# An attention-then-MLP kernel: four 64x64 transposes at a time, beta's transpose moved back, and a planner with other ScalarE and VectorE times

## The chip, the cores and the metric

The kernel runs on one core of one Trainium2 chip. The metric is the device time of one execution in microseconds (us); the time of the kernel before is the median of three runs, 304.22 us (304.19, 304.22 and 305.46). About 0.5% (1.5 us) is what a measurement of this kernel can tell from no change.

A core has TensorE (PE; its weight loads are shown apart as PEld), VectorE (DVE), ScalarE (ACT), GpSimd (POOL) and SyncE (SP), each with its own queue of instructions that run in order. Engines wait for one another by semaphores. POOL and SP issue nearly all DMAs here.

## The reference

Sliding-window attention over 8 batches and 8 heads (576 positions of 64 elements), followed by an MLP with a gated activation on the 4608 resulting tokens:

```python
scores = scale * np.matmul(q, k.transpose(0, 1, 3, 2))
mask_plain = (rel >= 0) & (rel < window)                                  # heads 0 to 3, window 32
mask_dil = (rel >= 0) & (rel < window * dilation) & (rel % dilation == 0) # heads 4 to 7, dilation 4
attn = softmax(scores where the mask holds)
x = np.matmul(attn, v), heads side by side: [4608, 512]
h = x @ w_in                                                              # [4608, 2048]
g = h * (1.0 / (1.0 + np.exp(-beta * h)))
out = g @ w_out                                                           # [4608, 512]
```

## The kernel before

The MLP is done in 9 tiles of 512 tokens. For a tile, the first product (line 868) makes 16 blocks of hidden units with four matmuls each; ACT takes a tanh of each block (line 877, scaled by half of beta), DVE forms the gate (line 882), and the second product (line 903) makes four blocks of 128 tokens with 16 matmuls each, which go out by way of `osb`. Input arrives in `xT`, the attention's output with features on partitions. Attention runs one batch at a time; batch b must be done before the tiles of tokens that it covers. For the first two batches `xT` is made by PE transposes (lines 807, 822 and 837), later by DMA.

For the first three batches (`DIRECT = 3`) keys and queries are loaded by DMA with a cast to bf16 into `st`, then transposed on PE, and copied out of PSUM by ACT or DVE:

- the dilated heads 4 to 7 (names KD0, KD1, QD0, QD1) by six transposes of 96 rows each (line 466) into `dk` and `dq`;
- the plain heads 0 to 3 (KP0, KP1, QP0, QP1) by 18 transposes each of a 64x64 piece (line 473) into `kT` and `qT`. Index i in 0 and 1 picks a pair of heads; the two heads of a pair lie on partitions 0 to 63 and 64 to 127 of `st`, and stay there in the output. KP0 and KP1 are two planned steps, each with its own PSUM bank.

Scores are made for the dilated heads at line 664, for the tail of the sequence at line 633 and for the plain heads at line 728; ACT takes the exponentials (line 600); values follow at lines 769, 785 and 754, and DVE divides by the sums (lines 619 and 620) into `xdm`, `xsp` and `xdt`. In batch 0 the mask is added in PSUM by matmuls with an identity (lines 654, 714 and 717); in the others it is multiplied after the exponential, on POOL or DVE (line 604).

The first keys (dilated, batch 0) come by SP's queue in float32 into the space of `g` and are cast by ACT and DVE; beta follows on the same queue. All other loads of the first 60 us go through POOL's queue in the order of its instructions: queries and keys of batch 0, its values, `w_in` in three parts, keys and queries of batch 1, `w_out` in two parts (8 of the 16 weight blocks each), and then values of batch 1 and the loads of batch 2.

No order is written by hand. A planner (`Plan`, above line 175) holds every step as an operation with a cost per engine, its dependencies and a due time `vt`. It walks through a modelled time: an engine is free again when its last operation has used up its cost (`free[e] = s + d`), and among the steps that can start then, the one that is due first is issued. `NUDGE` shifts the start that the planner sees for single steps, by the step's number, and so changes its choices. Where PE would stand idle by the plan, it puts in a filler matmul on zeros (line 1015). What comes out is a fixed order on each engine; on the chip each instruction runs when its engine reaches it and its semaphores allow it. The planner's costs are not times of the chip, and a change of any cost can move work in the whole program.

Beta's 16x128 array is transposed by one PE instruction (line 951), which needs its DMA and a small identity (`ident_f`) that POOL makes; DVE halves the result (line 953). Its due time of -1.4 lets the planner place it early: ahead of the batch 0 additions at line 654 and of all transposes of keys.

Of the kernel before, what the change touches and what calls it, by code (L numbers as in the profile page):

```python
# [36 lines left out]
class Plan:  # L37
# [3 lines left out]

    CAPS = {"h": 3, "p": 4, "o": 2, "z": 4, "a": 8, "s": 5, "w": 6}
    SWITCH = 95
    NUDGE = {32: -900, 54: 400, 98: -900, 188: -60, 192: -150, 263: -400, 287: 400, 292: -400, 294: 60,
        296: -150, 299: -60, 313: 900, 338: -400, 369: -150, 403: 400, 411: 900, 424: 400, 427: -150,
        527: -400, 770: -150, 970: -900, 977: -900, 988: -400, 1057: -60}
    LAT = {"PE": 210, "ACT": 45, "DVE": 45, "POOL": 60, "SP": 0}
    NEAR = {"PE": 40, "ACT": 60, "DVE": 60, "POOL": 60, "SP": 0}

    def __init__(self, banks):  # L50
# [9 lines left out]
    def run(self, filler=None, filler_until=0.0):  # L60
# [36 lines left out]
        while n_left:  # L97
            best = None
            near = {}
            for o in avail:  # L100
                base = o.ready
                at = {e: max([free[e], base] + [t for x, t in o.group.read.items() if x != e]
                             if o.group is not None and e != "PE" else [free[e], base]) for e, d in o.engs}
                if o.sbuf:
                    at = {e: max(t, port["DVE" if e == "POOL" else "POOL"]) for e, t in at.items()}
                fin = min(at[e] + d for e, d in o.engs)
                for e, d in o.engs:
                    start = at[e]
                    if start + d > fin + 100:
                        continue  # L110
                    if o.dma and len(lanes[e]) >= 8:
                        start = max(start, lanes[e][-8])
                    if o.acquire is not None:
                        start = bank_at(o.acquire, start)
                        if start is None:
                            continue
                    near.setdefault(e, []).append((start, o, d))
            picks = []
            for e, c in near.items():
                first = min(s + o.bias for s, o, _ in c)  # L120
                s, o, d = min((x for x in c if x[0] + x[1].bias <= first + self.NEAR[e]), key=lambda x: (x[1].vt, x[0]))
                picks.append((s, o.vt, e, o, d))
            assert picks, "no work can start"
            s, _, e, o, d = min(picks, key=lambda x: (x[0], x[1]))
            if filler is not None and s <= filler_until and free["PE"] + 300 < s:
                now = free["PE"]
                open_banks = {x.bank for x in held.values()}
                spare = [b for b, t in bank_free.items() if b not in open_banks and t <= now]
                if spare:
                    filler(max(spare, key=lambda b: -bank_free[b]))  # L130
                free["PE"] = now + 225
                halves = False
                continue
            for g in o.acquire or ():
                open_banks = {x.bank for x in held.values()}
                g.bank = min((b for b, t in bank_free.items() if b not in open_banks and t <= s + 1e-6),
                             key=lambda b: -bank_free[b])
                held[id(g)] = g
                g.left = len(g.users)
            o.fn(e)  # L140
            if e == "PE" and o.halves != halves:
                halves = o.halves
                d += self.SWITCH
            free[e] = s + d
            if o.sbuf:
                port[e] = s + d
            o.start, o.end = s, s + d + self.LAT[e]
            if o.group is not None and e != "PE":
                o.group.read[e] = o.end
            if o.dma:  # L150
                at = max(dma_free[e], s + d + 900)
                other = max(dma_free.values()) - at
                dma_free[e] = at + o.dma + max(0.0, min(o.dma, other))
                o.end = dma_free[e] + (o.lat or 1100)
                lanes[e].append(o.end)
            avail.remove(o)
            n_left -= 1
            for x in o.next:
                x.waits -= 1
                x.ready = max(x.ready, o.end)  # L160
                if not x.waits:
                    avail.append(x)
            for g in list(held.values()):
                if o in g.users:
                    g.left -= 1
                    if not g.left:
                        del held[id(g)]
                        g.release = max(u.end for u in g.users)
                        bank_free[g.bank] = g.release
                        ends.append(g)  # L170
            ends[:] = [g for g in ends if g.release > s - 5000]
# [9 lines left out]
def kernel(  # L181
# [10 lines left out]
    nc = tc.nc  # L192
# [199 lines left out]
    def load(queue, args, deps, vt, kb, rate=.4, issue=750, lat=1100):  # L392
        return plan.op(
            [(queue, issue)],
            lambda e: dma(queue, *args), deps, vt, dma=kb * 1024 / rate / 1000, lat=lat)

    def direct_qk(b, z, h0, deps, vt):
        rows, n, dst = ((2 * GD, RD, std) if h0 else (P, RP, stp))
        src = bass.AP(tensor=(k, q)[z].tensor, offset=(k, q)[z][b, h0].offset,
                      ap=[[n * D, rows], [2 * S * D, 2], [1, n * D]])  # L400
        return load("POOL", (dst[z], src), deps, vt, 576, .41 if b else .33, lat=1100 if b else 1500)

    def first_keys():

# [53 lines left out]

    def t_transposes(g, z, kind, i):
        if kind == "D":
            tp = bank(g, BF16)[:, 0:S].rearrange("p (s x g) -> p s x g", s=3, x=2)
            for s_ in range(3):
                for x in range(2):
                    nc.tensor.transpose(tp[:, s_, x], std[z][:, x, (2 * s_ + i) * P:(2 * s_ + i + 1) * P],  # L466
                                        ident_b[0:2 * GD, 0:2 * GD])
        else:
            tp = bank(g, BF16)[:, 0:S].rearrange("p (j g) -> p j g", j=RP)
            for j in range(RP):  # L470
                for h in range(2):
                    rows = slice(64 * h, 64 * h + 64)
                    nc.tensor.transpose(tp[rows, j], stp[z][rows, i, j * D:(j + 1) * D], ident_b[rows, rows])  # L473

    def at_once(x, i, h):

# [13 lines left out]
            last[key] = []  # L490

    xcopy = []

    def back_dma(b, j, vt_of, vdone):

# [33 lines left out]
    def attention(b, ld, names, vts):  # L529
# [2 lines left out]
        vt_of = dict(zip(names, vts))  # L532
        kv = b % 2
        if b < DIRECT:
            for n in [x for x in names if x[0] in "KQ"]:
                z, kind, i = "KQ".index(n[0]), n[1], int(n[2])
                vt = vt_of[n]
                g = Group("a")
                srcs = ld["qk", z, 0 if kind == "P" else 4]
                srcs = srcs if isinstance(srcs, list) else [srcs]  # L540
                tr = plan.op([("PE", (18 * mm(64) if kind == "P" else 6 * mm(QT)))],
                             lambda e, g=g, z=z, kind=kind, i=i: t_transposes(g, z, kind, i),
                             srcs + [ident], vt, acquire=g)
                used(("st", z), tr)
                def evac(e, g=g, z=z, kind=kind, i=i):
                    tp = bank(g, BF16)[:, 0:S]
                    if kind == "P":
# [11 lines left out]

        def mixed(e):  # L560
            copy(e, dkt[kv], dk[kv][:, :, :, CT - KTL:].rearrange("p r h k -> p h k r"))
        o = plan.op([("DVE", 450), ("POOL", 550)], mixed,
                    (steps["KD0"] + steps["KD1"] if b < DIRECT else ready["D"][0:1]) + war(("dkt", kv)), vt_of["T"] - .01, sbuf=True)
        used(("dk", kv, 0), o)
        used(("dk", kv, 1), o)
# [31 lines left out]
        def exp_and_mask(key, sop, g, vt, n, sc, w, m, tiles):  # L597
# [4 lines left out]
            if b >= ADDED or key == ("T",):  # L602
                def mask(e):
                    E[e].tensor_tensor(out=w(), in0=w(), in1=m(), op=ALU.mult)  # L604
                ex = plan.op([("POOL", 170 + 2.2 * n), ("DVE", 160 + .8 * n)], mask,
                             [ex] + [mask_tail if key == ("T",) else mask_ops["D" if key[0] in (2, 3) else "n"]],
                             vt, sbuf=True)
            wrote(*tiles)
# [16 lines left out]
        for name in [n for n in names if n[0] in "ST"]:  # L625
# [112 lines left out]
            for n, x in enumerate(xs):  # L738
                for h in range(2):
                    exp_and_mask((x, j, h), sop, gs[2 * n + h], vt, 3 * QT,  # L740
                                 lambda g=gs[2 * n + h]: bank(g)[:, 0:3 * QT].rearrange("p (a n) -> p a n", a=3),
                                 lambda x=x, j=j, h=h: pt[x][:, 6 * j:6 * j + 6].rearrange(
                                     "p (a h) n -> p h a n", h=2)[:, h, :, 0:QT],
                                 lambda j=j: mask_n[:, 1 + j:4 + j],
                                 [("pt", x, i) for i in range(3 * j, 3 * j + 3)])
        for name in [n for n in names if n[0] in "VU"]:
# [211 lines left out]
    vts = [-3 + 2 * i / len(first) for i in range(len(first))] + [-3, -2.5]  # L958
    vts[first.index("T"):len(first)] = [.2,.35,.45,.5]
    attention(0, ld[0], names0, vts)  # L960

    def xready(lo, hi, kts=range(NKT)):
        return [o for ks, a, b, o in xcopy if a < hi and b > lo and set(kts) & set(ks)]
# [85 lines left out]
```

The softmax here doesn't subtract the row's maximum and nothing guards it: scores larger than these inputs give would overflow.

## Time and profile before

| what | value |
|---|---|
| median of the runs | 304.22 us |
| span of the profiled execution, first to last instruction | 302.8 us |
| PE busy | 292.8 us, 97% |
| DVE busy | 187.8 us, 62% |
| ACT busy | 170.3 us, 56% |
| POOL busy | 88.5 us, 29% |
| DMA moved | 41.98 MB |

The profile gives one execution's span; the runs' times also hold what lies around the span, 1.4 us by the median. A row of a timeline gives the start in us from the span's start, the time it took, engine, source line, operation, out<-in by the program's names, shapes and how many instructions were merged; in brackets the engine's idle time before it and what ended it. A matmul's time holds the way through the array, so merged rows overlap a little. Some matmul records are missing in a trace: a row of 7 matmuls at line 868 can stand for 8.

### The profile page before, as it was taken

Reading aid. Unit: us, or ns where it says so; the run is one execution under the profiler, and the core shown is the slowest. Engines: PE = TensorE matmul, PEld = TensorE weight load, DVE = VectorE, ACT = ScalarE, POOL = GpSimd, SP = SyncE. Lnnn points to the kernel's source line nnn. Section 1 sums busy time; section 2 is a strip of 40 time slices with the busy share of each in tenths; the row PEclk is TensorE's granted clock in tenths of the full one; section 3 lists DMA queues with packets and bytes.
Section 4 is the critical chain, followed back from the end, with each engine's and each line's share of the span. In section 5 each row is a group of like instructions: output and inputs, shape, how many; then the busy total and the mean of one; then the engine's idle time right before and its main releaser. Section 6 shows DMA issues by size and latency. Waiting matters only on the chain.

```text
span 302.8 us, 5972 instructions
## 1 busy us (share of the span) xinstructions
PE 292.8 (97%) x2271; PEld 150.7 (50%) x2307; DVE 187.8 (62%) x424; ACT 170.3 (56%) x306; POOL 88.5 (29%) x126
## 2 busy tenths in 40 slices
PE   7989999999999999999999999999999999999995
PEld 4756555544554444445544454455544444444454
DVE  4777877688867837777677467577746544343300
ACT  3658974856745737383476447646465544554411
POOL 8997263762236137200631055200000000000000
PEclk9999999999999999999999999999999999999999
DMA  7999999799769999995699989996160100010122
GB/s 161 182 209 202 206 177 211 140 133 176 197 153 190 181 213 168 179 187 130 107 189 164 160 208 184 144 212 163 27 167 1 37 36 35 35 37 35 52 86 71
DMA packets 111248, 41.98 MB, mean 139 GB/s; under 512 B 87620, under 2 KB 104596, under 8 KB 111220
## 3 DMA queue, kind: packets, MB, share of 16 engines
q0 software_dynamic: 60336, 18.58, 58.7%
q1 hardware_dynamic: 50740, 22.95, 35.5%
q8 instruction: 18, 0.29, 0.4%
q10 hardware_dynamic: 144, 0.07, 0.1%
q14 instruction: 10, 0.08, 0.1%
HBM read 37.76 MB, written 18.87 MB: 187 GB/s over the span
## 4 chain that ended last, share of the span: by engine, by line
PE 89%; DVE 6%; issue 2%; DMA 1%; ACT 0%; SPq 0%; DVEq 0%
PE bank L903 40%; PE bank L868 39%; DVE g L882 2%; PE bank L785 2%; DMA beta_row<-in_moe_beta_dram 1%; PE bank L664 1%; PE bank L769 1%; PE bank L692 1%; PE bank L466 1%; PE bank L473 1%; DVE xdm L620 1%; DVE ptt L604 1%; PE bank L654 1%; PE bank L754 1%; PE bank L728 1%
## 5 line engine op out<-in xcount | busy, mean ns | idle before, releaser
L877 ACT ACTIVATE tnh<-bank,beta_half 128x512 bf16<-128x512 f32 x144 | 97.6, 690 | 71.4 <-PE bank L868 68.6
L903 PE MATMUL bank<-w_out_bf,g 128*128 128x512 bf16 (+2 forms) x588 | 136.2, 367 | 1.6 <-issue 0.8
L868 PE MATMUL bank<-xT,w_in_bf 128*128 128x512 bf16 (+1 forms) x568 | 136.1, 376 | 1.0 <-issue 0.2
L882 DVE SCALAR_TENSOR_TENSOR g<-tnh,bank 128x512 bf16<-128x512 bf16 x144 | 97.3, 686 | 62.2 <-ACT tnh L877 61.4
L868 PEld LDWEIGHTS <-w_in_bf 128*128 128x128 bf16 x584 | 55.4, 98 | 61.8 <-issue 0.4
L903 PEld LDWEIGHTS <-g 128*128 128x128 bf16 x608 | 54.9, 98 | 56.5
L918 ACT ACTIVATE osb<-bank 128x512 f32<-128x512 f32 (+1 forms) x34 | 20.0, 588 | 31.2 <-PE bank L903 30.4
L600 ACT ACTIVATE pt<-bank 128x384 bf16<-128x384 f32 (+1 forms) x54 | 20.4, 466 | 6.4 <-PE bank L692 4.3
L604 DVE TENSOR_TENSOR pt<-pt,mask_n 128x384 bf16<-128x384 bf16 (+1 forms) x41 | 15.1, 381 | 8.7 <-ACT pt L600 8.1
L600 ACT ACTIVATE ptd<-bank 128x512 bf16<-128x512 f32 x32 | 16.6, 602 | 6.6 <-PE bank L664 6.6
L620 DVE TENSOR_TENSOR xsp<-bank,rcp 96x384 bf16<-96x384 f32 x32 | 17.7, 554 | 1.1
L619 DVE RECIPROCAL rcp<-bank 128x4 f32<-128x4 f32 (+2 forms) x72 | 12.8, 178 | 6.6 <-PE bank L785 3.4
L390 POOL DMA_DIRECT2D vp<-in_v_dram x9 | 15.3, 1696 | 0.4 <-DVE dkt L239 0.4
L620 DVE TENSOR_TENSOR xdm<-bank,rcp 128x256 bf16<-128x256 f32 x32 | 13.6, 425 | 1.1
L390 POOL DMA_DIRECT2D s<-in_q_dram x10 | 13.6, 1356 | 0.0
L390 POOL DMA_DIRECT2D vt<-in_v_dram x16 | 13.4, 1007 | 0.2 <-issue 0.2
L920 DVE TENSOR_SCALAR osb<-bank 128x512 f32<-128x512 f32 (+2 forms) x4 | 2.1, 522 | 18.1 <-PE bank L903 18.1
L604 DVE TENSOR_TENSOR ptd<-ptd,mask_d 128x512 bf16<-128x512 bf16 x27 | 10.8, 422 | 2.2 <-ACT ptd L600 1.7
L981 POOL COPY pace<-xT 1x2 bf16<-1x2 bf16 x4 | 0.9, 213 | 38.0 <-DMA xT<-x 38.0
L239 POOL COPY vd<-st 128x1024 bf16<-128x1024 bf16 x5 | 5.3, 1053 | 22.3 <-DMA st<-in_v_dram 22.3
L390 POOL DMA_DIRECT2D s<-in_k_dram x10 | 11.1, 1115 | 1.0 <-issue 0.8
L785 PEld LDWEIGHTS <-pt 128*128 128x128 bf16 x192 | 8.8, 97 | 4.7
(110 smaller groups left out, 188.2 us busy)
## 6 DMA issues: line engine op xcount, KB each, us to landing
out_dram<-osb SPq DMA_DIRECT2D x35, 256.0 KB, 3.4
s<-in_q_dram POOLq DMA_DIRECT2D x10, 288.0 KB, 9.4
s<-in_k_dram POOLq DMA_DIRECT2D x10, 288.0 KB, 6.5
w_out_bf<-in_moe_w_out_dram POOLq DMA_DIRECT2D x2, 1024.0 KB, 16.8
vp<-in_v_dram POOLq DMA_DIRECT2D x7, 288.0 KB, 17.1
st<-in_q_dram POOLq DMA_DIRECT2D x6, 288.0 KB, 9.8
x<-xsp SPq DMA_DIRECT2D x12, 144.0 KB, 4.5
st<-in_k_dram POOLq DMA_DIRECT2D x5, 288.0 KB, 11.2
```

The costliest lines, as they stand in the source:

```text
L239: (nc.scalar.copy if e == "ACT" else E[e].tensor_copy)(out=out, in_=in_)
L390: {"POOL": nc.gpsimd, "SP": nc.sync}[queue].dma_start(out=out, in_=in_)
L600: nc.scalar.activation(out=w(), in_=sc(), func=ACT.Exp, scale=SCALE)
L604: E[e].tensor_tensor(out=w(), in0=w(), in1=m(), op=ALU.mult)
L619: nc.vector.reciprocal(out=r, in_=p[..., D])
L620: nc.vector.tensor_tensor(out=dst, in0=p[..., 0:D], in1=r.unsqueeze(len(p.shape) - 1).to_broadcast(list(p.shape[:-1]) + [D]), op=ALU.mult)
L785: nc.tensor.matmul(pv[:, a, h2, :], lhsT=lhs, rhs=vp[kv][:, (2 * x + h2) * NI + 3 * j + a, 0:D + 1], start=True, stop=True)
L868: nc.tensor.matmul(bank(g)[:, a:z], lhsT=w_in_bf[:, kt, fb * P:(fb + 1) * P], rhs=xT[:, kt, xo + a:xo + z], start=(i == 0 and kt == kts[0] ...
L877: nc.scalar.activation(out=th[:, 0:n], in_=bank(g)[:, 0:n], func=ACT.Tanh, scale=beta_half[:, fb:fb + 1])
L882: nc.vector.scalar_tensor_tensor(out=g_t[t % 2][:, fb, c0:c0 + n], in0=th[:, 0:n], scalar=1.0, in1=bank(g)[:, 0:n], op0=ALU.add, op1=ALU.mult)
L903: nc.tensor.matmul(bank(g)[:, lo:hi], lhsT=g_t[t % 2][:, fb, tb * P:(tb + 1) * P], rhs=w_out_bf[:, fb, lo:hi], start=(fb == 0), stop=(fb = ...
L918: nc.scalar.mul(out=ob[:, lo:hi], in_=bank(g)[:, lo:hi], mul=0.5)
```

## The change

Four things are changed.

1. The plain transposes of both head pairs (i = 0 and 1) of keys, or of queries, become one planned step with two PSUM banks. Its 36 transposes are ordered piece by piece over the two pairs, and the second pair's heads change sides: head h of pair x is written to the partitions `half[h ^ x]`. Four transposes in a row so use four different combinations of input half and output half. The copies out of PSUM stay as they are, but wait for the whole step. The exponentials of the plain scores of batches 0 to 2 write to the place of the swapped head.
2. Beta's transpose gets the third of the recorded transposes, that of KD1, the third name in batch 0's list, as one more dependency (`bt.deps.append(turned[2])`).
3. The planner's view of costs: an ACT operation over 250 ns frees its engine 105 ns earlier and a DVE operation 80 ns earlier (`LAP`); a multiplication by the mask and the copy to `dkt` on DVE are cheaper; the latency of batch 0's loads is 1000 in place of 1500.
4. The table `NUDGE` has other entries.

Number and shapes of PE's instructions stay, except for one filler (29 in place of 30). From POOL to DVE go three mask products of plain scores, four copies into `vd` and one into `vp`; one copy to `dkt` goes from DVE to POOL. Some copies out of PSUM change places between ACT and DVE.

```diff
-    NUDGE = {32: -900, 54: 400, 98: -900, 188: -60, ...}
+    NUDGE = {7: -150, 12: 150, 16: -400, 45: -400, 59: -900, ...}
+    LAP = {"PE": 0, "ACT": 105, "DVE": 80, "POOL": 0, "SP": 0}
...
-            free[e] = s + d
+            free[e] = s + d - (self.LAP[e] if d > 250 else 0)
...
-        return load("POOL", (dst[z], src), deps, vt, 576, .41 if b else .33, lat=1100 if b else 1500)
+        return load("POOL", (dst[z], src), deps, vt, 576, .41 if b else .33, lat=1100 if b else 1000)
...
-            for j in range(RP):
-                for h in range(2):
-                    rows = slice(64 * h, 64 * h + 64)
-                    nc.tensor.transpose(tp[rows, j], stp[z][rows, i, j * D:(j + 1) * D], ident_b[rows, rows])
+    def t_quarters(gs, z):
+
+        tps = [bank(g, BF16)[:, 0:S].rearrange("p (j g) -> p j g", j=RP) for g in gs]
+        half = [slice(64 * h, 64 * h + 64) for h in range(2)]
+        for j in range(RP):
+            for x in range(2):
+                for h in range(2):
+                    nc.tensor.transpose(tps[x][half[h ^ x], j], stp[z][half[h], x, j * D:(j + 1) * D],
+                                        ident_b[half[h], half[h]])
...
-                tr = plan.op([("PE", (18 * mm(64) if kind == "P" else 6 * mm(QT)))],
-                             lambda e, g=g, z=z, kind=kind, i=i: t_transposes(g, z, kind, i),
-                             srcs + [ident], vt, acquire=g)
-                used(("st", z), tr)
+                if kind == "P" and i == 0:
+                    gs = [Group("a") for _ in range(2)]
+                    tr = plan.op([("PE", 18 * 36)], lambda e, gs=gs, z=z: t_quarters(gs, z),
+                                 srcs + [ident], vt, acquire=gs)
+                    quarters[z] = gs, tr
+                    used(("st", z), tr)
+                elif kind == "D":
+                    g = Group("a")
+                    tr = plan.op([("PE", 6 * mm(QT))], lambda e, g=g, z=z, i=i: t_transposes(g, z, i),
+                                 srcs + [ident], vt, acquire=g)
+                    used(("st", z), tr)
+                turned.append(tr)
+                if kind == "P":
+                    g, tr = quarters[z][0][i], quarters[z][1]
...
-        o = plan.op([("DVE", 450), ("POOL", 550)], mixed,
+        o = plan.op([("DVE", 360), ("POOL", 550)], mixed,
...
-                ex = plan.op([("POOL", 170 + 2.2 * n), ("DVE", 160 + .8 * n)], mask,
+                ex = plan.op([("POOL", 170 + 2.2 * n), ("DVE", 160 + .53 * n)], mask,
...
-                                     "p (a h) n -> p h a n", h=2)[:, h, :, 0:QT],
+                                     "p (a h) n -> p h a n", h=2)[:, h ^ (x if b < DIRECT else 0), :, 0:QT],
...
+    bt.deps.append(turned[2])
```

## The prediction

> **What bounds the kernel now.** I read the page first, then a table of stretches, then the timelines of PE and DVE, then the loads. On the page, PE is busy and carries the chain of waits; of the other engines none is near it.
>
> ```profile
> PE 292.8 (97%) x2271; PEld 150.7 (50%) x2307; DVE 187.8 (62%) x424; ACT 170.3 (56%) x306; POOL 88.5 (29%) x126
> PE 89%; DVE 6%; issue 2%; DMA 1%; ACT 0%; SPq 0%; DVEq 0%
> ```
>
> The stretches (PE first, clock and GB/s last) say where PE is not full. Of the 10 us of idle time 3.4 lie in the first 20 us and 0.7 to 0.8 in each of the next two stretches; the last row's 4.9 are mostly records that the trace lacks.
>
> ```profile
> 0.00:20.00 20.00, 16.63 (x232) 11.80 (x234) 13.27 (x45) 10.55 (x23) 17.80 (x37) 1.00 1.18 180
> 20.00:42.00 22.00, 21.27 (x252) 12.50 (x255) 16.34 (x39) 17.87 (x36) 13.82 (x22) 1.00 1.33 202
> 42.00:66.00 24.00, 23.22 (x265) 12.88 (x267) 19.46 (x45) 15.43 (x33) 13.20 (x15) 1.00 1.40 170
> 66.00:110.00 44.00, 43.52 (x326) 21.66 (x333) 33.31 (x73) 27.24 (x50) 14.50 (x18) 1.00 1.33 176
> 110.00:303.00 193.00, 188.13 (x1202) 91.84 (x1222) 105.46 (x225) 99.17 (x167) 29.22 (x35) 1.00 0.74 114
> ```
>
> PE's timeline shows what the first 22 us hold: fillers, a wait for beta, the additions (line 654), transposes and scores of batch 0. Only at 22.12 does the first product run without a break.
>
> ```profile
> 1.13 3.81 PE L1015 MATMUL bank<-zero 128*128 128x256 bf16 x17 [1.13 <-DVE warm L298]
> 5.74 0.26 PE L951 MATMUL bank<-ident_f,beta_row 16*128 16x16 f32 x1 [0.80 <-DMA beta_row<-in_moe_beta_dram]
> 5.93 1.89 PE L654 MATMUL bank<-add_d,ident_b 128*128 128x512 bf16 x4
> 7.61 1.17 PE L466 MATMUL bank<-ident_b,st 96*128 96x96 bf16 x12
> 9.75 0.82 PE L1015 MATMUL bank<-zero 128*128 128x256 bf16 x5
> 11.49 0.62 PE L664 MATMUL bank<-dq,dk 64*128 64x128 bf16 x16
> 22.12 4.45 PE L868 MATMUL bank<-xT,w_in_bf 128*128 128x512 bf16 x26
> 31.36 1.32 PE L473 MATMUL bank<-ident_b,st 64*64 64x64 bf16 x72
> 36.79 1.03 PE L903 MATMUL bank<-w_out_bf,g 128*128 128x512 bf16 x4
> 44.66 1.89 PE L903 MATMUL bank<-w_out_bf,g 128*128 128x512 bf16 x8
> ```
>
> DVE's timeline shows the chain that ends this stage: from 8.81 to the last `xsp`, which ends at 21.92, DVE is busy 11.49 of 13.11 us.
>
> ```profile
> 5.45 0.56 DVE L239 CAST st<-g 96x768 bf16<-96x768 f32 x1 [1.29 <-DMA g<-in_k_dram]
> 8.81 0.76 DVE L239 COPY dk<-bank 128x576 bf16<-128x576 bf16 x1 [2.60 <-PE bank L466]
> 10.29 0.74 DVE L239 COPY dq<-bank 128x576 bf16<-128x576 bf16 x1
> 21.37 0.55 DVE L620 TENSOR_TENSOR xsp<-bank,rcp 96x384 bf16<-96x384 f32 x1
> ```
>
> The last view is of `w_out`'s loads. They are issued at 19.24 and 25.62 and land 17.1 and 16.6 us later, so at about 36.4 and 42.2. The page's slices have 130 to 210 GB/s all through that time: POOL's queue is full, and a load lands when its turn comes.
>
> ```profile
> L390 POOL DMA_DIRECT2D w_out_bf<-in_moe_w_out_dram x2: 887/896/904, 19.2 to 25.6; - x2
> DMA to landing us min/median/max: 16.6/16.8/17.1
> ```
>
> **The change part by part.** The new order, as the planner leaves it, is laid out with durations of these rows.
>
> *Start.* Ten fillers, then the four additions, then seven fillers stand ahead of the first transposes; beta's transpose stands behind the transposes of plain queries. POOL makes `add_d` and the large identity right behind its first load and `ident_f` much later, so the additions can start near 3.4, as the ten fillers end (1.13 + 10 x 0.213). With 4 x 0.43 and 7 x 0.213 the first transposes start at 6.65 in place of 7.61; the keys don't stop this, ACT's cast ends at 6.28. If the first query load, issued 0.7 earlier, slows the keys' load, up to 0.3 of that is covered. The beta wait of 0.80 goes for nothing else: its load lands at 5.6 and is wanted near 11.5, and DVE's halving (0.17) only has to precede the first tanh, at 23.2.
>
> *To the first product.* The transposes of dilated keys and queries follow each other: 24 in 1.92 at the pace of 7.61 (12 in 0.96), so `dq` starts on DVE at 8.85, not 10.29. From there DVE has, by its rows: `dq` 0.74, `dkt` 0.69, `qt` 0.48, `kT` twice 1.42 and `qT` once 0.71, `vd` 0.74, beta 0.17, `vp` twice 0.64, four `xdm` of 0.55 and four `xsp` of 0.69. That is 10.55, and the last `xsp` ends at 19.4, 2.5 before 21.92. What could hold it up is not late: the plain queries land at 10.4 (estimate: issue 3.60, and behind two loads of 1.4 to 2.2 each), values at 12 to 14. ACT took the whole stage with idle time. PE's two waits for an exponential's bank (0.3 to 0.4 each) lie beside this chain. Ends: 1.5, if the first copies or `vd` wait a us longer; 3.2, if the transposes run at the fast pace (12 in 0.68 at 29.62, with 0.2 of pipe).
>
> That pace is the next point. The page's clock row shows 9 throughout, yet a filler takes 0.213 until 9.95 and 0.109 later (five in 0.82, two of them slow). The Trainium skill, page "TensorE: Matmul & The Clock Gate", Part 1, has the same two paces and says that about 3.4 us of sustained work, in a window that runs by itself, lift the gate. The 3.6 us of fillers here did not, and the fast pace came 4.2 us after the beta wait. By the rule the new start, without that gap, could be fast from 6.6 on, and this stage would give 3.2; the sum uses 2.5.
>
> *From 20 to 42.* This lead isn't all kept. The new order ends the first tile's first product and all scores of batch 1 before the first block at line 903 (36.4), and after 16 matmuls of that kind it meets the wait for the second half of `w_out`, at 42.2. By then the old order had 4 matmuls of line 868, 4 of line 903, six scores and four transposes of `xdm` less: 8 x 0.2157 (20 of line 868 in 4.32 in the chain) + 0.24 + 0.22 = 2.2. So the lead there is 2.2 if PE stands waiting. It will: besides the 2.5 it saves the four fillers near 26.5 (0.44). Only an earlier landing adds to this. The query load moves up by 0.72 (the two `ident_f` steps and its wait), the next two move back by about 0.4 behind `add_d`, which the full queue covers. Ends 0 and 0.7; I take 0.3, since SP's key load shares the engines until 4.6.
>
> *Plain transposes.* 72 take 1.32 less 0.19 of pipe: 31 ns a pair, so two already run at once. Four at once would save half of 0.56 for each of the six steps; two run beside the DVE chain, two ahead of the `w_out` wait, so only batch 2's two count: 0 to 0.56. Batch 2's steps also came in three pieces between other work (0.11 twice at the change of shape). I take 0.5 for both. The Trainium skill, "TensorEngine Tiling (Array Packing)", names four independent 64x64 tiles but says that a change of tiling mode drains the array, and for row tiles that they cannot use the same bank at the same time. The 31 ns a pair with both halves in one bank speak against the second; no row shows four. By the page's drain the gain would be nothing, by its four tiles 0.56.
>
> *Later.* Batch 2's dilated queries now load last: POOL issues them behind the plain loads, `vd` and two `vt`, after 45.5 (when `vt` of batch 1 lands) in place of 36.95. With the median of 9.8 they land near 55.3; their transposes stand behind 16 matmuls that start near 52, at 55.8. Cost 0 to 2, taken 0.3. The three masks, four `vd` (0.74) and one `vp` that DVE takes over are 4.5 us on an engine with 115 us free; PE's idle time for DVE is 0.5 (line 728 near 65), which may go or come: 0. The tail has both last quarters on ACT (0.28 each, the first ends at 299.87): 0.1 at most. From 110 on PE is at 0.2157 a matmul in both.
>
> Sum: 2.2 + 0.3 + 0.5 - 0.3 = 2.7 off the span of 302.8, so 300.1, and with the 1.4 around it **301.5**.
>
> **The rivals.** *The lead is used up (same).* The lead is only as good as the loads behind it. If batch 2's queries cost the full 2, or the first stage loses 1.5 more by a wait for a bank and PE meets `w_out` late, 0.7 to 1.2 remain: 303.3. For it: the order of loads is changed and POOL waits in order (5.4 at 36.95 alone). Against: slack of 6 us, since 28 matmuls of line 903 of tile 0 were left when tile 1 began at 51.6.
>
> *Four tiles collide (slower).* If each change of output half stops the array for 0.1, as at the changes of shape, 18 stops in each step cost 1.8; four steps behind the first stage are 7.2, two of them in part covered by the `w_out` wait. From 45 ns a stop on (2.7 + 0.5 saved, over 72 stops; more where covered) it is no gain; at 0.1, 304.2 - 2.2 + 5.5 = 307.5. Against: pairs on different halves already run 31 ns apart without a stop.
>
> *All goes well (faster still).* Landings 0.7 earlier, four at once, queries in time, the 0.5 at 65 gone: 2.2 + 0.7 + 0.8 + 0.5 = 4.2, so 300.0.
>
> *The quarters don't run at once, and nothing stops.* Then 0.3 to 0.5 less: 301.9, inside the forecast.
>
> **How the numbers follow.** Forecast 0.53, well 0.14, used up 0.19, collision 0.14. More than 0.5% (below 302.7) is faster: 0.67; same 0.19; slower 0.14. The forecast's own range is 300.6 to 302.7; with the good case and most of the used-up one it is 299.9 to 304.4, which leaves the collision and a little at both ends out.
>
> **What would show it.** Beta's row behind line 728's first neighbours, no 0.80 wait; first transposes at 6.7; last `xsp` at 19 to 19.5; a PE wait for `w_out` near 42; 72 plain transposes in less than 1.32. It is wrong if the last `xsp` stays past 20.5, `w_out` lands later than 42.5, or PE waits near 56 for queries.

## The result, and the profile after

The changed kernel takes 305.5 us (median; 304.48 to 307.49) beside 304.3 us (303.81 to 305.46) for the kernel before: a ratio of 1.0042 with a 95% interval of 1.0032 to 1.0051, so 1.3 us slower where 2.7 us faster was predicted. The profiled execution's span is 304.1 us in place of 302.8.

The page of the changed kernel has PE busy for as long as before (292.8 us; the trace of the kernel before lacks 36 records of matmuls, this one none), but its chain of waits leaves PE far oftener, for DMA above all:

```profile
PE 292.8 (96%) x2306; PEld 146.4 (48%) x2306; DVE 192.3 (63%) x435; ACT 168.1 (55%) x302; POOL 81.9 (27%) x119
PE 75%; DMA 10%; DVE 7%; POOL 3%; ACT 2%; issue 1%; SPq 1%; POOLq 0%; ACTq 0%
```

The start is what the prediction drew. PE's timeline has the additions at 3.73, the first transposes at 6.19 (before: 7.61), the quarter steps (line 477) at 0.48 each, beta at 11.60 without a wait, and the first product without a break from 19.39 (before: 22.12):

```profile
3.73 1.58 PE L671 MATMUL bank<-add_d,ident_b 128*128 128x512 bf16 x4 [0.27 <-POOL ident_b masks.py:199]
5.15 0.93 PE L1033 MATMUL bank<-zero 128*128 128x256 bf16 x7
6.19 1.45 PE L467 MATMUL bank<-ident_b,st 96*128 96x96 bf16 x24
8.71 0.48 PE L477 MATMUL bank<-ident_b,st 64*64 64x64 bf16 x36
11.60 0.23 PE L968 MATMUL bank<-ident_f,beta_row 16*128 16x16 f32 x1
19.39 4.93 PE L885 MATMUL bank<-xT,w_in_bf 128*128 128x288 bf16 x30
```

To see where that lead goes, PE's work is counted in both traces: every instruction by its columns (0.2157 us for 512; half for transposes of 64x64 pieces and for scores, of which two run at once), without fillers, up to a time. The changed kernel's work less that of the kernel before is its lead in us: 2.2 at 22 us, 2.5 at 40, 0.1 at 48, 1.2 at 62, 1.6 at 104, and then -0.9 at 125. From there it stays near -1.0. Records that a trace lacks have to be filled in, so a lead is good to a few tenths. It is lost twice: between 40 and 48 (1.5 of this is back by 104), and, with 2.6 us, between 107 and 119.

The first loss is on PE's timeline. All blocks of tile 0's first product are done; PE has fillers (line 1033) while the transposes of `xdm` (line 839) wait for DVE:

```profile
42.05 0.49 PE L1033 MATMUL bank<-zero 128*128 128x256 bf16 x3
43.01 0.38 PE L839 MATMUL bank<-ident_b,xdm 128*128 128x128 bf16 x4 [0.47 <-DVE xdm L637]
43.23 0.49 PE L1033 MATMUL bank<-zero 128*128 128x256 bf16 x3
44.11 0.38 PE L839 MATMUL bank<-ident_b,xdm 128*128 128x128 bf16 x4 [0.39 <-DVE xdm L637]
106.53 1.03 PE L920 MATMUL bank<-w_out_bf,g 128*128 128x512 bf16 x4
108.78 1.89 PE L885 MATMUL bank<-xT,w_in_bf 128*128 128x512 bf16 x8 [1.23 <-DMA xT<-x]
115.69 1.03 PE L920 MATMUL bank<-w_out_bf,g 128*128 128x512 bf16 x4
118.00 1.02 PE L885 MATMUL bank<-xT,w_in_bf 128*128 128x512 bf16 x4 [1.28 <-DVE g L899]
```

The last four rows are the second loss. At 107.5 the new order begins tile 3's first product (line 885) right after tile 1's last block, and waits 1.23 for `xT` of batch 3; the old order had 36 matmuls of line 903 there, from 107.20 to 115.13. At 116.7 PE waits 1.28 for a gate. DVE's and POOL's timelines show what the gate stood behind; the last two rows are PE's and DVE's of the kernel before:

```profile
113.15 0.69 DVE L899 SCALAR_TENSOR_TENSOR g<-tnh,bank 128x512 bf16<-128x512 bf16 x1 [1.04 <-ACT tnh L894]
113.87 2.37 DVE L241 COPY vp<-vp 32x1280 bf16<-32x1280 bf16 x1
116.27 0.95 DVE L241 COPY qt<-dq 64x128 bf16<-64x128 bf16 x2
117.26 0.69 DVE L899 SCALAR_TENSOR_TENSOR g<-tnh,bank 128x512 bf16<-128x512 bf16 x1
```

```profile
113.68 2.13 POOL L392 DMA_DIRECT2D s<-in_q_dram  x1
114.77 2.23 POOL L392 DMA_DIRECT2D vp<-in_v_dram  x1
```

```profile
107.20 7.93 PE L903 MATMUL bank<-w_out_bf,g 128*128 128x512 bf16 x36
115.03 0.48 DVE L239 COPY vp<-vp 32x1280 bf16<-32x1280 bf16 x1
```

The copy inside `vp` for batch 4 takes 2.37; in the kernel before it took 0.48, at 115.03. At that moment, in the changed kernel, POOL issues these two loads.

### The profile page after: what moved, and what is told of

The parts are those of the page before. It is cut to its first block, busy times and chain, and to the rows that moved or that the text cites. A ratio compares the mean times of both kernels' runs of the same rounds, so it can differ in the third digit from the quotient of the medians.

```text
span 304.1 us, 6006 instructions
## 1 busy us (share of the span) xinstructions
PE 292.8 (96%) x2306; PEld 146.4 (48%) x2306; DVE 192.3 (63%) x435; ACT 168.1 (55%) x302; POOL 81.9 (27%) x119
## 4 chain that ended last, share of the span: by engine, by line
PE 75%; DMA 10%; DVE 7%; POOL 3%; ACT 2%; issue 1%; SPq 1%; POOLq 0%; ACTq 0%
PE bank L920 35%; PE bank L885 33%; DMA w_in_bf<-in_moe_w_in_dram 4%; DMA xT<-x 3%; DMA x<-xsp 2%; DVE g L899 2%; PE bank L802 1%; DVE pt L621 1%; PE bank L709 1%; PE bank L786 1%; DVE vp L241 1%; PE bank L681 1%; DVE xsp L637 1%; DVE xdm L637 1%; PE bank L467 1%
## 5 line engine op out<-in xcount | busy, mean ns | idle before, releaser
L885 PE MATMUL bank<-xT,w_in_bf 128*128 128x512 bf16 (+2 forms) x584 | 139.7, 376 | 2.9 <-DVE g L899 1.3
L920 PE MATMUL bank<-w_out_bf,g 128*128 128x512 bf16 (+2 forms) x608 | 141.3, 368 | 0.5 <-ACT pt L617 0.5
L885 PEld LDWEIGHTS <-w_in_bf 128*128 128x128 bf16 x584 | 54.7, 98 | 63.8 <-issue 3.5
L935 ACT ACTIVATE osb<-bank 128x512 f32<-128x512 f32 (+1 forms) x33 | 19.0, 579 | 23.1 <-PE bank L920 22.6
L392 POOL DMA_DIRECT2D vt<-in_v_dram x16 | 14.4, 1030 | 1.4 <-DMA vp<-in_v_dram 1.4
L636 DVE RECIPROCAL rcp<-bank 96x6 f32<-96x6 f32 (+2 forms) x72 | 12.8, 178 | 2.0 <-PE bank L802 1.2
L937 DVE TENSOR_SCALAR osb<-bank 128x512 f32<-128x512 f32 (+1 forms) x5 | 3.2, 638 | 14.9 <-PE bank L920 14.9
L241 ACT COPY xT<-bank 128x288 bf16<-128x288 bf16 (+2 forms) x16 | 5.0, 369 | 11.2 <-PE bank L824 4.8
```

The source lines that it names most:

```text
L241: (nc.scalar.copy if e == "ACT" else E[e].tensor_copy)(out=out, in_=in_)
L392: {"POOL": nc.gpsimd, "SP": nc.sync}[queue].dma_start(out=out, in_=in_)
L636: nc.vector.reciprocal(out=r, in_=p[..., D])
L885: nc.tensor.matmul(bank(g)[:, a:z], lhsT=w_in_bf[:, kt, fb * P:(fb + 1) * P], rhs=xT[:, kt, xo + a:xo + z], start=(i == 0 and kt == kts[0] ...
L920: nc.tensor.matmul(bank(g)[:, lo:hi], lhsT=g_t[t % 2][:, fb, tb * P:(tb + 1) * P], rhs=w_out_bf[:, fb, lo:hi], start=(fb == 0), stop=(fb = ...
L935: nc.scalar.mul(out=ob[:, lo:hi], in_=bank(g)[:, lo:hi], mul=0.5)
```

## The experiments

The theory (A): the early lead is real, and the new order loses it in a few late waits, which the order alone makes. The rival (B): loads and copies of fixed times cap the lead whatever the order. For most experiments the planner's choices (step, engine, PSUM banks) are written out as a list that the kernel issues one by one, and the list is edited. In the diffs, H t f is block f of tile t's first product, O t b.p is part p (four matmuls) of token block b of its second product. Ratios are to the kernel before, with 95% intervals.

**1. The wait for `xT` alone.**

```diff
  PE   O 1 3.3
+ PE   O 2 0.1, O 2 0.2
  PE   H 3 0, H 3 1
- PE   O 2 0.1
+ PE   O 2 0.3                    (later groups of O 2 move up by two places)
```

> The changed kernel with its own order, except that two groups of four matmuls of tile 2's second product (parts 1 and 2 of the first token block) stand ahead of tile 3's first matmuls, and the groups behind them move up by two places. Theory A, the lead is real and is lost in two late waits: the wait of 1.23 for the second half of batch 3's xT near 107.5 is gone or under 0.3, the wait for a gate near 118 stays; the time falls by about 1.0 to 1.2, to about 304.4 (ratio to the kernel before about 1.000). Rival B, PE is held back by loads and copies anyway, and the wait only shows where: the time stays within 0.4 of the changed kernel's (ratio 1.003 to 1.005) and a wait of about 1 turns up later.

Measured: 1.0049 (1.0036 to 1.0063), no gain. The wait for `xT` is gone and the lead is 2.0 at 115 us, but PE then stands 1.14 for the gate at 117.9, and 0.69 at 139.3, where the groups moved away had covered tile 3's last gate. POOL issues batch 5's loads when this same `xT` lands, so DVE's slow copy stays where it was. So 0.69 of the 1.23 that PE gains at 107 is waited for again at 139.

```profile
117.90 1.02 PE L885 MATMUL bank<-xT,w_in_bf 128*128 128x512 bf16 x4 [1.14 <-DVE g L899]
139.26 2.10 PE L920 MATMUL bank<-w_out_bf,g 128*128 128x512 bf16 x9 [0.69 <-DVE g L899]
```

**2. The copy inside `vp` later on DVE.**

```diff
  DVE  gate 3 2
- DVE  copy inside vp, batch 4
  DVE  qt copies, gate 3 3, dkt, gate 3 4, gate 3 5
+ DVE  copy inside vp, batch 4
```

> The changed kernel with its own order, except that DVE's copy inside vp for batch 4 (32x1280) stands behind the gates of tile 3's blocks 3, 4 and 5 in place of ahead of them. Theory A: the wait of 1.28 for a gate near 118 is gone or under 0.3, the wait for xT at 107.5 stays; the time falls by about 1.0 to 1.3, to about 304.4 (ratio about 1.000). It also says whether the copy's 2.37 us belong to the copy or to the moment: at its new place, with POOL not issuing transfers of vp, it should take 0.5; if it takes 2 us again, the copy itself is slow in this layout. Rival B: no gain over 0.4, another late instruction of DVE takes the place.

Measured: 1.0013 (0.9995 to 1.0032), 0.9 us less than the changed kernel; the wait for `xT` is 1.1, that for the gate gone. DVE's timeline decides the side question: the copy takes 0.48 at its new place, and the `qt` copies that now stand at 113.66 take 2.19.

```profile
113.66 2.19 DVE L241 COPY qt<-dq 64x128 bf16<-64x128 bf16 x2
115.88 0.69 DVE L899 SCALAR_TENSOR_TENSOR g<-tnh,bank 128x512 bf16<-128x512 bf16 x1
119.12 0.48 DVE L241 COPY vp<-vp 32x1280 bf16<-32x1280 bf16 x1
```

**3. Both edits.**

```diff
  PE   O 1 3.3
+ PE   O 2 0.1, O 2 0.2
  PE   H 3 0, H 3 1
...
- DVE  copy inside vp, batch 4      (now behind gate 3 5)
```

> Both edits of the two kernels before in one. Theory A: 2.2 to 2.5 less than the changed kernel, about 303.0 (ratio about 0.996 to 0.997), and the lead at 124, 140 and 250 us is about 1.5 over the kernel before. Rival B: at most 0.5 less, ratio 1.002 or more. If each edit alone gives its part and both together less than the sum, the second wait had been hiding behind the first.

Measured: 1.0019 (0.9998 to 1.0039), 0.7 us less than the changed kernel and not the 2.2 expected: no more than edit 2 gave. Both waits are gone (lead 0.9 at 115, 0.8 at 119), but this execution came to 107 us with only 0.6, and 0.69 goes at 139 as in experiment 1.

**4. The old order from 107.5 us.**

```diff
  (the changed kernel's list up to O 1 3.3)
- the rest of its list
+ the rest in the order and on the engines of the kernel before
```

> The changed kernel up to the last group of tile 1's second product (107.5 us), and from there every instruction on every engine in the order, and on the engine, of the kernel before. Theory A, the loss is one of the late order alone: the lead of 1.5 at 104 us stays to the end, the time is 302.7 to 303.2 (ratio 0.995 to 0.997). Rival B, the lead was borrowed from work that has to be done later (copies, masks, transfers), whatever the order: the time is not below 304.0, and PE meets new waits between 107 and 140.

Measured: 0.9991 (0.9974 to 1.0008). 1.5 us less than the changed kernel, so the loss is one of the late order; but nothing is gained on the kernel before. The time lies between the two expectations. PE's lead in this profile was 1.1 at 104, 0.6 at 125 and 0.4 at the end.

**5. Four at once alone, and taken back alone.** The first kernel has the quarter steps in the old order. The second has the new order without them:

```diff
-                    nc.tensor.transpose(tps[x][half[h ^ x], j], stp[z][half[h], x, j * D:(j + 1) * D],
+                    nc.tensor.transpose(tps[x][half[h], j], stp[z][half[h], x, j * D:(j + 1) * D],
...
-                                     "p (a h) n -> p h a n", h=2)[:, h ^ (x if b < DIRECT else 0), :, 0:QT],
+                                     "p (a h) n -> p h a n", h=2)[:, h, :, 0:QT],
```

> The kernel before with one part of the change alone: the plain transposes are made four at a time (one step per keys or queries, at the place of the first of the two old steps); the order and the engines of all other steps, beta's place among them, are those of the kernel before. If the four-at-once step is a gain by itself (36 took 0.48 in the changed kernel's profile, 72 took 1.32 before), PE saves about 0.25 to 0.3 a step in batches 1 and 2, so the time falls by 0.3 to 1.0 (ratio 0.997 to 0.999). If it only shortens a step whose copies are waited for anyway, no change within 0.2 (ratio 1.000). If the copies, which now wait for the whole step, come later and hold PE, it is up to 0.5 slower (1.001 to 1.002).

> The changed kernel with that one part taken back: the same order and the same 36 transposes a step, but each head stays on its side, so that only two different combinations of input half and output half follow one another. If four at once is worth what the rows say, a step takes 0.76 to 0.9 in place of 0.48 and the time rises by 0 to 0.5 over the changed kernel (ratio 1.004 to 1.006 to the kernel before; the lead at 36 us falls by about 1.0, and part of that was lost in the waits behind it anyway). If the four were the cause of the loss, the time falls below 304.5 (ratio 1.001 or less).

Measured: 0.9991 (0.9981 to 1.0001) and 1.0070 (1.0047 to 1.0094). Four at once makes a step shorter: with two at once all six steps take 0.75 or 0.76 in place of 0.48, as in these rows of the second kernel's PE timeline. The second kernel is 0.85 us over the changed kernel by the ratios, which is hardly more than their intervals leave open, and 1.2 by the medians.

```profile
9.27 0.76 PE L477 MATMUL bank<-ident_b,st 64*64 64x64 bf16 x36
30.91 0.75 PE L477 MATMUL bank<-ident_b,st 64*64 64x64 bf16 x36
```

In the old order the step gives a lead of 1.5 at 22 us, of which 0.4 is left at 26: there PE waits 0.80 ahead of batch 1's first transposes.

```profile
26.01 0.43 PE L467 MATMUL bank<-ident_b,st 96*128 96x96 bf16 x6 [0.80 <-DVE g L899]
```

**6. Beta's transpose alone.**

```diff
- PE   beta's transpose
  PE   additions, KD0, KD1
+ PE   beta's transpose
```

> The kernel before with one part of the change alone: beta's transpose stands behind the transposes of the second dilated keys on PE, and its halving behind their copy on DVE; all else as before. PE's wait of 0.80 for beta is gone, so the additions and the first transposes come up to 0.8 earlier (6.9 in place of 7.6). If that start is kept, the time is 303.5 or less (ratio under 0.998). If the next load, the keys of batch 1 near 26, caps it, as it did the start of four at a time in the old order, nothing is left: ratio 0.999 to 1.001.

Measured: 0.9988 (0.9976 to 1.0000). The unbroken first product starts at 20.77 in place of 22.12, and again little is left (lead 0.6 at 26 and 0.3 from 40 on): PE waits for batch 1's keys.

```profile
20.77 4.45 PE L868 MATMUL bank<-xT,w_in_bf 128*128 128x512 bf16 x26
25.76 0.43 PE L466 MATMUL bank<-ident_b,st 96*128 96x96 bf16 x6 [0.33 <-DMA st<-in_k_dram]
```

**7. The new start, then the old order.**

```diff
  (the changed kernel's list up to the first product, about 20 us)
- the rest of its list
+ the rest in the order and on the engines of the kernel before
```

> The changed kernel up to the first product's beginning (about 20 us), and from there the order and the engines of the kernel before, with the four-at-once step in batches 1 and 2. It keeps the start's lead of about 3.3 and none of the new late waits. Theory A, the lead is real and the new order from 20 us on loses it: 302.0 to 303.2 (ratio 0.993 to 0.997). Rival B, loads cap the lead whatever the order (third part of w_in near 25, second half of w_out at 42.2, xT): PE's work in front of the kernel before falls under 1.0 by 48 us, and the time is 303.5 or more (ratio over 0.998).

Measured: 1.0015 (0.9999 to 1.0030). Here rival B is right. The lead of 2.5 at 22 us meets the load of batch 1's keys, which lands at 25.6, and is 0.6 at 26 and 0.5 at 48:

```profile
25.66 0.43 PE L467 MATMUL bank<-ident_b,st 96*128 96x96 bf16 x6 [1.67 <-DMA st<-in_k_dram]
```

**8. The late order alone.**

```diff
- the changed kernel's list up to O 1 3.3
+ the same steps in the order and on the engines of the kernel before (beta's too)
  (the rest of the changed kernel's list)
```

> The counterpart of the kernel that had the old order from 107.5: the four-at-once step and the old order up to the end of tile 1's second product, and from there the changed kernel's order and engines. If the late order by itself costs the loss, this kernel, with hardly any lead (0.4 at 104 us), is 0.5 to 1.5 slower than the one with the old order throughout: ratio 1.001 to 1.004, with a wait for a gate near 118 behind a copy inside vp or a qt copy of about 2.2. The wait for xT at 107.5 is shorter than 1.23 by what PE comes later, about 0.2 to 0.5. If the late order only costs where PE comes early, the ratio is that of the old order, 0.998 to 1.000.

Measured: 1.0107 (1.0089 to 1.0125), slower than either theory asked for. With 0.9 of lead at 104 us it waits 1.7 for `xT` and 1.3 for the gate, as its table of PE's waits says (wait, total us, times, longest):

```profile
PE bank L885 <- DMA xT<-x: 1.7, 1, 1.7
PE bank L885 <- DVE g L899: 1.3, 1, 1.3
```

With experiments 4 and 5 this makes a square of orders up to 107.5 us and from there, all four with four at once: old and old 0.9991, new and old 0.9991, new and new 1.0042, old and new 1.0107. The new late order costs 3.5 us after the old early order and 1.6 after the new one. The new early order is worth 2.0 us with the new late order and nothing measurable with the old.

**9. The early losses taken out as well.**

```diff
- PE   six fillers around the transposes of xdm (42 us)
+ PE   O 0 3.0, O 0 3.1
...
- DVE  copy inside vp, batch 3; masks; divisions
+ DVE  masks; divisions; copy inside vp, batch 3
  (old order from 107.5 us, as in experiment 4)
```

> The changed kernel with the four waits that the profiles show taken out, each by the order alone: near 42 two groups of four matmuls of the second product stand in the place of six fillers on zeros, so PE has work while DVE makes xdm; the copy inside vp for batch 3 stands behind the divisions on DVE, so that it doesn't hold DVE until its load lands near 79.5; from 107.5 on the order is that of the kernel before. Theory A: the lead is 2 to 3 at 48 and 66 us, nothing over 0.5 is lost at 80, 107 and 117, and the time is 301.3 to 302.7 (ratio 0.990 to 0.995). Rival B: the lead is cut by some other wait before 110, and the time is 303.2 or more (ratio over 0.997).

Measured: 0.9981 (0.9964 to 0.9999), less gain than theory A asked for. The lead is 3.0 at 48, 3.1 at 62 and 2.7 at 104 us, so the loss at 42 was PE's order and not `w_out`'s landing. Then 2.1 go between 112 and 117, in the old late order: DVE's `dkt` copy holds the next eviction until its load has landed at 112.35 (PE waits 0.49), and the `qt` copies fall into POOL's issues and take 2.15 (PE waits 1.46).

```profile
114.47 2.15 DVE L241 COPY qt<-dq 64x128 bf16<-64x128 bf16 x2
```

**10. Batch 4's copies moved too.** The edits of experiment 9, and:

```diff
- DVE  dkt, eviction of O 2 0, copy inside vp, qt copies
+ DVE  eviction of O 2 0, qt copies, dkt; copy inside vp behind the first division
...
- PE   O 2 1.0, O 2 0.1, O 2 1.1, O 2 0.2, O 2 1.2, O 2 0.3, O 2 1.3
+ PE   O 2 1.0, O 2 0.1, O 2 0.2, O 2 0.3, O 2 1.1, O 2 1.2, O 2 1.3
+ PE   O 0 2.1 ahead of batch 1's transposes of xsp
```

> The kernel without the waits near 42, 80 and 107.5, in which the last profile showed the lead of 2.7 lost between 112 and 117 behind DVE's copies of batch 4 (dkt held by its load, qt held at 2.15 while POOL issued loads), with those moved too: on DVE the eviction of tile 2's first block and the two qt copies stand ahead of dkt, and the copy inside vp for batch 4 behind the first division; on PE the first block's groups come before the second's, and one group stands ahead of batch 1's transposes of xsp near 48.7. Theory A: the lead of 2.5 to 3 is kept beyond 120 us, and the time is 301.0 to 302.2 (ratio 0.989 to 0.994). Rival B: a load of batch 4 or later holds PE in place of the copies, the lead falls under 1.2 by 125 us, and the time is about 303.4 as in the kernel without this edit (ratio 0.997 to 0.999).

Measured: 302.43 us, 0.9940 (0.9921 to 0.9959): faster than both kernels. In its profile no late wait of PE over 0.2 is left after 100 us, but 1.2 of the lead went between 80 and 84, where DVE's `xdm` waits for an earlier store of `xdm`; 0.8 of lead is left at 200. The profiled execution was the slowest of the six (303.67), so the others may have kept more. Theory A's mechanism holds, its size only in part.

```profile
81.23 0.42 DVE L637 TENSOR_TENSOR xdm<-bank,rcp 128x256 bf16<-128x256 f32 x1 [0.93 <-DMA x<-xdm]
```

**11. POOL's two loads behind the gate.** Every engine's order is the changed kernel's.

```diff
+    late = plan.ops[805].fn
+    def after_gate(e):
+        nc.gpsimd.tensor_copy(out=pace[:], in_=g_t[1][0:1, 3, 0:2])
+        return late(e)
+    plan.ops[805].fn = after_gate
     plan.run(filler, 80000.0)
```

> The changed kernel with every engine's order as it is, and one small POOL instruction added: ahead of POOL's last two loads of batch 5 (plain queries and vp, issued at 113.68 and 114.77 in the changed kernel) POOL reads two elements of the gate of tile 3's block 3, so that they are issued only after that gate. Theory A, the copy inside vp (2.37) and the qt copies (0.95) are slow because POOL issues these loads at that moment: the copy takes 0.5, the qt copies 0.4, the gate comes at about 115.5 in place of 117.26, and PE's wait near 118 falls from 1.28 to under 0.3; the wait for xT at 107.5 stays; the time falls by about 0.8 to 1.2 (ratio 1.000 to 1.002). Theory B, the copy is slow for another reason (its layout, DVE's own state, the other DMA traffic): it stays over 1.5, and so do the wait and the time (ratio 1.003 to 1.005).

Measured: 1.0002 (0.9978 to 1.0027), 1.2 us less than the changed kernel (the two intervals leave 0.4 to 2.0), with the wait for `xT` left in (1.20). DVE's and POOL's timelines:

```profile
113.61 0.63 DVE L241 COPY vp<-vp 32x1280 bf16<-32x1280 bf16 x1
114.26 0.39 DVE L241 COPY qt<-dq 64x128 bf16<-64x128 bf16 x2
114.68 0.69 DVE L899 SCALAR_TENSOR_TENSOR g<-tnh,bank 128x512 bf16<-128x512 bf16 x1
```

```profile
115.50 0.18 POOL L1038 COPY pace<-g 1x2 bf16<-1x2 bf16 x1 [1.57 <-DVE g L899]
116.00 1.59 POOL L392 DMA_DIRECT2D s<-in_q_dram  x1 [0.32 <-issue]
117.10 1.67 POOL L392 DMA_DIRECT2D vp<-in_v_dram  x1
```

The copy takes 0.63 at the same moment and in the same place of DVE's order, the gate comes at 114.68, and PE has no wait at 117. So the copy was slow because POOL issued loads.

The leads side by side, from one profiled execution of each kernel (us of PE work over the kernel before):

| at us | 22 | 26 | 40 | 48 | 72 | 104 | 125 | 200 |
|---|---|---|---|---|---|---|---|---|
| changed kernel | 2.2 | 1.7 | 2.5 | 0.1 | 1.8 | 1.6 | -0.9 | -0.9 |
| four at once, old order | 1.5 | 0.4 | 0.7 | 0.0 | 0.4 | 0.4 | 0.4 | 0.4 |
| old order from 20 | 2.5 | 0.6 | 1.1 | 0.5 | 0.8 | 0.6 | 0.6 | 0.8 |
| old order from 107.5 | 2.6 | 2.5 | 3.2 | 1.4 | 2.8 | 1.1 | 0.6 | 0.4 |
| new order from 107.5 | 1.7 | 0.6 | 1.2 | 0.8 | 0.9 | 0.9 | -2.3 | -2.5 |
| loads behind the gate | 2.6 | 2.6 | 3.4 | 1.2 | 2.6 | 1.7 | 0.3 | 0.6 |
| experiment 9 | 2.6 | 2.5 | 3.2 | 3.0 | 3.1 | 2.7 | 0.6 | 0.4 |
| experiment 10 | 2.4 | 2.3 | 2.5 | 2.3 | 2.6 | 1.1 | 1.0 | 0.8 |

## Why the prediction was wrong, step by step

*Start and first product: right.* The last `xsp` was put at 19.4 and ends at 19.19; the lead at 22 us is 2.2, where the sum had 2.5 for this stage; the first transposes start at 6.19, not 6.65, because the fast pace came with the fillers at 5.15 (seven in 0.93) in place of 10. PE had worked since 1.14 with one gap of 0.27. That is what the Trainium skill, page "TensorE: Matmul & The Clock Gate", Part 1, lets expect of about 3.4 us of sustained work, and the 24 transposes took 1.45 in place of the 1.92 of the sum.

*20 to 42: right in size, wrong in what comes next.* 2.2 to 2.5 of lead at 40 to 42 was predicted, 2.5 was there at 40 and 1.7 at 42. But PE did not stand for `w_out`: it stood for `xdm`, twice, with fillers between. The step took the `w_out` landing for the cap and never laid out DVE's chain of masks, values and divisions behind it. The landing itself came at 42.8 in this profile (issued at 26.82, 16.0 to landing), where 0.3 earlier than 42.2 had been counted on and later than 42.5 was named as a sign of being wrong; no row of PE waits for it. Of the lead 0.1 to 1.6 was left at 48 us in the seven profiles of kernels with this order there. Experiment 9 keeps 3.0 by putting eight other matmuls in that place.

*Plain transposes: right in sign.* 0.5 was taken. A step takes 0.28 less, and taking it back costs 0.85 us by the ratios (1.2 by the medians), with about 0.8 either way, so 0.5 isn't refuted. The rival with four colliding tiles falls: 36 in 0.48, no stop at a change of half, and this agrees with the Trainium skill's page "TensorEngine Tiling (Array Packing)", section "64×64 Mode (4 tiles)", which lists four tiles, one for each combination of input half and output half.

*Batch 2's late queries: 0.3 taken, nothing seen;* PE's table of waits of the changed kernel has none for them.

*"Later": the step that failed.* It said that the masks, `vd` copies and the `vp` copy taken over by DVE are "4.5 us on an engine with 115 us free" and cost 0, and that "from 110 on PE is at 0.2157 a matmul in both". Idle time of an engine was taken for room. What counts is who stands behind the new instruction, and when. The copy inside `vp` of batch 4 was on DVE in both kernels, but the new order put it ahead of gates that PE's banks waited for, at the moment of POOL's loads; the copy inside `vp` of batch 3, taken over from POOL, held DVE for 2.0 until its load had landed, near 79.5 and 80.0, in experiments 2 and 4 (PE waited 1.46 and 1.45 there). And the order of PE itself, tile 3 ahead of tile 2's second product, was not laid out after 66 us at all, so the wait for `xT` was missed. The loss is 2.6 in the profile between 107 and 119; by the square the late order costs 1.6 us after this early order and 3.5 after the old one.

The rival "the lead is used up" named the right kind of mechanism, a lead only as good as the loads behind it, but at the wrong loads (batch 2's queries). In the old order it is most of the story: a wait near 26 us takes most of the lead, for batch 1's keys in experiments 6 and 7, for a gate in 5. No rival had an order that costs time by itself, which is why the slower side had been left to the colliding tiles.

Not settled: why experiment 1 gains nothing in time although its profiled span is 0.7 shorter than the changed kernel's (that execution was the fastest of its five), and how much of the lead of experiment 10 can be kept at 80 us.

## What to carry to other kernels

When a change lets a planner choose again, lay out the whole of its new order: the stage that was meant to gain was the part that came out right. A lead on the bounding engine is worth only what the next load's landing, or the next in-order engine that stands behind such a landing, lets through; list these landings with their slack before a start is counted as a gain. Before a copy is given to an engine with idle time, look at what stands behind it in that engine's order, and at what POOL is issuing at that moment.

## What the runs showed of the hardware

DVE's copies from SBUF to SBUF can be held up while POOL issues large loads. The `vp` copy takes 0.48 or 2.37, the two `qt` copies 0.4 or 2.2, and the slow ones end 2.3 to 2.6 us after POOL began the query load (113.68 and 116.24; 113.57 and 115.85; 114.14 and 116.62). It is the issuing and not the loads' traffic: in experiment 2 the `vp` copy took 0.48 at 119.12, with POOL idle and the DMA engines at 251 GB/s from 119 to 121. And not every issue does it: in the kernel before the copy took 0.48 at 115.03, while POOL issued two `vt` loads (114.37 to 116.38), and in experiment 4 it took 0.48 when it began at 113.96, just ahead of the query load at 113.98. The gates, with one input in PSUM, took 0.69 in the same stretch. The masks, with both inputs in SBUF, are hit too: three took 2.36 at 37.53 beside a POOL copy of `vd` that began at 37.91, and 0.91 in experiment 2, where that copy began as they ended. The Trainium skill, page "SBUF — State Buffer", section "Who interferes with whom", has a rule that fits: DVE's second pair of ports is GpSimd's, and when a DVE instruction uses it, whoever begins first holds it for a whole instruction, and the other is blocked and not slowed. That a lock of this kind is at work here is an inference; the runs show the times. The page tells of DVE holding up POOL's descriptors; here it is POOL that holds up DVE, and one added POOL instruction of 0.18 us was worth 1.2 us.

Kernels with the new start can spread more from run to run (experiment 11: 302.66 to 306.88; old order with four at once: 303.48 to 304.39). That they come closer to the landing of loads would explain it, but no run tested that.
